# One core, layer norm, a scan and a gated feed-forward: up weights loaded row tile by row tile

## The chip, the cores and the metric

The kernel runs on one NeuronCore of a Trainium2 chip. The metric is the device time of one execution in microseconds (us): 178.7 us is the median of three runs of the kernel before, which lie between 178.48 and 179.15. Lower is better. The engines are TensorE (PE, with its weight loads PEld), VectorE (DVE), ScalarE (ACT), GpSimd (POOL) and SyncE (SP), whose queue issues nearly all DMAs here.

## What is computed

x is [2048, 512] in bfloat16. It is normalised over its 512 columns, then goes through two branches whose results are multiplied and added to x:

```python
xn = _layernorm(x, axis=-1)
s = _A_ref(xn, ...)          # h = Lam_bar*h + B_bar xn_t, y = 2 Re(C h) + xn*Dskip
g = _silu(_B_ref(xn, w_gate, w_up, w_down))
return x + s * g

def _B_ref(x, w_gate, w_up, w_down):
    return (_gelu(x @ w_gate) * (x @ w_up)) @ w_down
```

Branch A is a complex diagonal recurrence over the 2048 rows with 512 states, branch B a feed-forward of 1376 hidden columns.

## The kernel before, in words

The 2048 rows are cut into four slabs of 512 (NS = 4), each slab into four row tiles of 128 (M = 4). The 512 input columns are four row tiles of the weights (KT = 4, called k, rows 0 to 3 here), and the 1376 hidden columns are three chunks CH: 512, 512 and 352. W1 = 512 and W2 = 1024 are the ends of the first two.

For slab 0 the centred rows are transposed on TensorE (head_t, lines 378 to 402) into xcT, which lies in the tile W, and the up and gate products read it with the row scale put on at eviction. up_rows (lines 454 to 465) is one matmul, for row tile m, weight row k and chunk c; the four k of one (m, c) accumulate in one PSUM bank, and the last evicts it through out_up (L471, ScalarE). first_w (L499) does all four k of one (m, c) at a stretch, for the up chunks that up_rows leaves and for the gate weights wg (first_gates). In the kernel before up_rows takes the two wide chunks alone, and the 352-column chunk of all four row tiles goes through first_w.

For slabs 1 to 3 the normed rows are transposed by a DMA (dma_t4, L436) into xnT, and gate_tile (L536, evictions L539) computes up and gate products. Down products are L564 (down_pair; their SiLU is L567), with the gated rows transposed by a DMA (at_t, L551) into atT. half (L615, evictions L617) is the input product of the recurrence with BT; the rotations (L627, L635, L639) and the scans (L646) follow on VectorE. y_part (L579, L585, L586) is the output product with the C matrices, the two element-wise steps and the store (L589).

Loads: load_x (L296) brings one row tile of slab 0, load_w (L287) a part of wu or wg, load_slab (L291) a whole slab of x, L762 and L763 the down weights, L314, L436, L551 and L807 are DMA transposes. Before any of them TensorE runs seven dummy matmuls (L375).

The order of all work is written out by hand: every piece is registered with Plan.add in program order, and Plan.run emits the pieces in the order of the table ORDER, with buffers and PSUM banks given by SLOTS (six banks "ps", two "pp"). Each engine executes its own instructions strictly in that order. Numbers such as the end and landing times given to dma_sp, costs and ranks are arguments that Plan.add takes and does not use. The DMAs of SP and ACT share eight completion semaphores in turn, so a DMA waits on SP's queue until the eighth DMA before it has landed.

The order of SP's first loads before: x tiles 0, 1, 2; wu row 0 in two 512 chunks; the 352 chunk of all four rows in one load; wu row 1 first chunk; x tile 3; wu row 1 second chunk, row 2 first chunk, row 3 both wide chunks in one, row 2 second chunk; wg columns 512 to 1375, wg columns 0 to 511; slab 1; Drow; then the transposes.

Of the kernel before, what the change touches and what calls it, by code (L numbers as in the profile page):

```python
# [51 lines left out]
    ),  # L52
    "pp": (
        0, 1, 0, 1, 0, 1, 0, 1, 0, 0, 0, 1, 0, 1, 0, 1, 0, 1, 0, 1, 1, 0, 1, 0, 1, 1, 1, 0, 0, 0, 0, 1, 1, 0, 1, 0, 1, 0, 1,
    ),
    "U": (
        0, 1, 0, 2, 0, 1, 0, 2,
    ),
    "g2": (
        5, 0, 1, 4, 3, 0, 4, 2, 2, 0, 1, 5, 3, 1, 4, 5,  # L60
    ),
    "at": (
        2, 0, 1, 3, 2, 1, 0, 0, 0, 1, 2, 3, 2, 3, 0, 1,
    ),
    "gtA": (
        0, 0, 1, 1, 0, 1, 0, 1, 1, 0, 0, 0, 1, 1, 0, 0,
    ),
    "gtB": (
        1, 1, 0, 0, 0, 0, 1, 1, 1, 0, 0, 0, 0, 1, 0, 1,
    ),  # L70
    "ubA": (
        0, 1, 0, 0, 1, 1, 1, 0, 0, 0, 1, 1,
    ),
    "ubB": (
        0, 0, 1, 1, 1, 0, 0, 1, 0, 0, 1, 0,
    ),
    "yg": (
        0, 0, 1, 1, 0, 1, 0, 1, 0, 1, 1, 0, 0, 0, 1, 0, 1, 0,
    ),
    "ot": (  # L80
        1, 1, 1, 0, 1, 0, 0, 0, 0, 0, 0, 1, 1, 0, 1, 0, 1,
    ),
    "sk": (
        2, 3, 0, 1, 5, 7, 4, 6, 0, 1, 3, 2, 5, 4, 6, 7,
    ),
    "atT": (
        0, 1, 3, 0, 1, 1, 3, 2, 0, 3, 2, 1, 1, 2, 3, 0,
# [61 lines left out]
def kernel(  # L149
# [140 lines left out]
    def load_slab(s, **kw):  # L290
        dma(SP, 0.8, 4.0, lambda: nc.sync.dma_start(out=x_tok[:, s * M : (s + 1) * M, :], in_=x_r[:, s * M : (s + 1) * M, :]),  # L291
            writes=[("x", s, m) for m in range(M)], svc=SLAB, **kw)
# [8 lines left out]
    load_x(2, 2.06, 3.75)  # L301
    load_w("wu", 0, 1, 0, W1, 2.53, 4.4)
    load_w("wu", 0, 1, W1, W2, 3.0, 4.95)
    load_w("wu", 1, 2, 0, W1, 3.47, 5.5)
    load_w("wu", 1, 2, W1, W2, 3.94, 6.05)
    load_x(3, 4.41, 6.6)
    load_w("wu", 2, 3, 0, W1, 4.88, 7.15)
    load_w("wu", 2, 3, W1, W2, 5.35, 7.7)
    load_w("wu", 3, 4, 0, W2, 5.82, 8.8)
    load_w("wu", 0, KT, W2, F, 6.29, 10.0)  # L310
    load_w("wg", 0, KT, W1, F, 6.76, 12.4)
    load_w("wg", 0, KT, 0, W1, 7.23, 14.0)
# [141 lines left out]
    def up_rows(m, k, c):  # L454

        a, b = CH[c]
        if (m, c) not in opened:
            opened[m, c] = bank(m == 3)
        key, ps = opened[m, c]

        def f():
            T.matmul(ps[:], lhsT=xcT[:, k, m * P : (m + 1) * P], rhs=wu[:, k, a:b], start=(k == 0), stop=(k == KT - 1))  # L462
        pe(1, 512, f, [("xcT", m, k // 2), ("wu", k, c)], [key])
        if k == KT - 1:
            out_up(m, c, ps, key)
# [90 lines left out]
    def down_pair(s, h):  # L556
        for m in (2 * h, 2 * h + 1):
            key, ps = bank()
            gT, iT = atTs[s, m]

            def f(iT=iT, ps=ps):
                for k in range(NFT):
                    fs = min(P, F - k * P)
                    T.matmul(ps[:], lhsT=atT[:fs, k, iT * P : (iT + 1) * P], rhs=wd[:fs, k, :], start=(k == 0), stop=(k == NFT - 1))  # L564
            pe(NFT, 512, f, [("atT", gT), "wd0", "wd"], [key])
            g, i = g2s[s, m] = pl.group("g2")
            acts(512, lambda i=i, ps=ps: act(out=g2[i][:], in_=ps[:], func=AF.Silu), [key], [("g2", g)], table="silu", rank=3.0)  # L567
# [165 lines left out]
    up_rows(0, 0, 0)  # L733
    up_rows(0, 0, 1)
    head_t(2)
    for c in range(2):
        up_rows(1, 0, c)
    up_rows(0, 1, 0)
    up_rows(1, 1, 0)
    for c in range(2):  # L740
        up_rows(2, 0, c)
    for m in range(2):
        up_rows(m, 1, 1)
    for c in range(2):
        up_rows(2, 1, c)
    head_t(3)
    for c in range(2):
        for m in range(3):
            up_rows(m, 2, c)
    for k in range(3):  # L750
        for c in range(2):
            up_rows(3, k, c)
    for m in range(M):
        for c in range(2):
            up_rows(m, 3, c)
    for m in range(M):
        first_w("wu", m, 2)
# [4 lines left out]
    dma(SP, 0.6, 6.7, lambda: nc.sync.dma_start(out=wd[:, 0 : NFT - 1, :], in_=wd_r), writes=["wd0"], after=sp_last, svc=(2, 3.7, 1.0))  # L762
# [60 lines left out]
    def norm(s):  # L823
        if s > 1:
            load_slab(s, after=turned)
# [94 lines left out]
```

## Time and profile before

| | us |
|---|---|
| median of three runs (178.48 to 179.15) | 178.7 |
| span of the profiled execution | 176.9 |
| TensorE busy | 172.1 |
| VectorE busy | 154.6 |
| ScalarE busy | 132.6 |
| GpSimd busy | 10.9 |

The time of a run goes from the start of the program to its end on the device; the span goes from the first to the last instruction of the profiled execution, and 1.8 us of the median lie around it. Busy times are sums over the instructions of an engine; matmuls are pipelined and their shown length is latency, so the distance from one start to the next is the better measure. A row of the timeline gives start, length, engine, line, operation, what it writes and reads, and the count; a row of the chain of waits gives start, length and what the end of the kernel hung on at that time. The clock that TensorE was granted is 1.00 in every stretch.

### The profile page before, as it was taken

The numbers are of one execution on the slowest core, as the hardware profiler recorded it, in microseconds if no ns is written. First come the engines' busy times: TensorE is split into PE (matmuls) and PEld (weight loads), VectorE is DVE, ScalarE is ACT, GpSimd is POOL, SyncE is SP. The second block draws the span as 40 slices with busy tenths as digits, with TensorE's granted clock in tenths as the row PEclk, the third lists the DMA queues.
The fourth block names the chain that finished last, engine by engine and source line by source line (L and its number), as shares of the span: only waits on it lengthen the run. The fifth ranks groups of instructions, "written<-read, shape, count | busy, mean of one in ns | idle before, by whom it ended". The sixth has DMA issues, their size and how long they took to land.

```text
span 176.9 us, 2418 instructions
## 1 busy us (share of the span) xinstructions
PE 172.1 (97%) x834; PEld 82.3 (47%) x849; DVE 154.6 (87%) x253; ACT 132.6 (75%) x246; POOL 10.9 (6%) x25
## 2 busy tenths in 40 slices
PE   8999999999999999999999999999999999999992
PEld 2554544454454444444444444444444444444451
DVE  3743799999999988999999699999999999999343
ACT  6679999989999999956697665735898860793310
POOL 2640500000200000011000000000000000000000
PEclk9999999999999999999999999999999999999999
DMA  5999999997092730040057050063007300550531
GB/s 150 285 347 247 160 288 189 305 217 158 8 193 43 138 62 4 0 82 0 0 115 150 2 111 0 0 126 70 0 11 154 87 0 4 129 123 0 113 119 30
DMA packets 48467, 18.66 MB, mean 105 GB/s; under 512 B 40296, under 2 KB 48328, under 8 KB 48456
## 3 DMA queue, kind: packets, MB, share of 16 engines
q1 hardware_dynamic: 48432, 18.52, 46.7%
q8 instruction: 6, 0.10, 0.2%
q14 instruction: 5, 0.04, 0.1%
q10 hardware_dynamic: 24, 0.00, 0.0%
HBM read 6.46 MB, written 2.10 MB: 48 GB/s over the span
## 4 chain that ended last, share of the span: by engine, by line
PE 94%; DMA 2%; SPq 1%; issue 1%; DVE 0%
PE bank L536 31%; PE bank L564 21%; PE bank L615 16%; PE bank L579 16%; PE bank L499 7%; PE bank L462 3%; DMA wu<-in_B_w_up_dram 2%; SPq L296 1%; SPq L287 0%; DVE yg L585 0%; DVE ot L586 0%; PE bank L400 0%
## 5 line engine op out<-in xcount | busy, mean ns | idle before, releaser
L536 PEld LDWEIGHTS <-xnT 128*128 128x128 bf16 x288 | 28.1, 98 | 29.4
L564 PE MATMUL bank<-wd,atT 128*128 128x512 bf16 (+1 forms) x174 | 40.2, 379 | 0.1
L536 PE MATMUL bank<-wu,xnT 128*128 128x512 bf16 (+1 forms) x140 | 31.9, 356 | 0.1
L536 PE MATMUL bank<-wg,xnT 128*128 128x512 bf16 (+1 forms) x139 | 31.7, 356 | 0.3
L615 PE MATMUL bank<-xnT,BT 128*128 128x512 bf16 x128 | 30.9, 379 | 0.1
L646 DVE TENSOR_TENSOR_SCAN Fs<-rho,ini,W 128x512 bf16<-128x512 f32 x24 | 29.8, 1272 | 0.1
L579 PE MATMUL bank<-C,hst 128*128 128x512 bf16 (+1 forms) x134 | 29.7, 366 | 0.1
L564 PEld LDWEIGHTS <-atT 128*128 128x128 bf16 (+1 forms) x176 | 17.2, 98 | 20.3
L539 ACT ACTIVATE ubA<-bank 128x512 bf16<-128x512 f32 x24 | 14.6, 614 | 8.8 <-PE bank L536 8.3
L617 ACT ACTIVATE U<-bank 128x512 bf16<-128x512 f32 x32 | 19.1, 622 | 1.7 <-PE bank L615 1.7
L579 PEld LDWEIGHTS <-hst 128*128 128x128 bf16 x136 | 13.3, 98 | 14.0
L615 PEld LDWEIGHTS <-BT 128*128 128x128 bf16 x128 | 12.5, 98 | 14.3
L627 DVE TENSOR_TENSOR Q<-U,tab 128x4096 bf16<-128x4096 bf16 x8 | 18.3, 2287 | 0.7 <-ACT tab L715 0.6
L539 ACT ACTIVATE gtA<-bank 128x512 bf16<-128x512 f32 x24 | 14.8, 616 | 5.3 <-PE bank L536 4.6
L627 DVE TENSOR_TENSOR Q<-Fs,tab 128x4096 bf16<-128x4096 bf16 x8 | 18.3, 2285 | 0.1
L567 ACT ACTIVATE g<-bank 128x512 f32<-128x512 f32 x16 | 9.2, 594 | 12.1 <-PE bank L564 12.1
L585 DVE TENSOR_TENSOR yg<-bank,g 128x512 bf16<-128x512 f32 (+1 forms) x17 | 11.1, 655 | 5.0 <-PE bank L579 4.6
L539 ACT ACTIVATE ubB<-bank 128x352 bf16<-128x352 f32 x12 | 5.7, 475 | 6.6 <-PE bank L536 5.5
L838 ACT ACTIVATE junk<-x_tok 128x512 bf16<-128x512 bf16 x16 | 10.2, 649 | 0.0
L499 PE MATMUL bank<-wg,W 128*128 128x512 bf16 (+1 forms) x47 | 9.7, 356 | 0.1
L843 ACT ACTIVATE xna<-x_tok,nb,rs 128x512 bf16<-128x512 bf16 x12 | 9.6, 876 | 0.0
L575 ACT ACTIVATE bank<-sk 128x512 f32<-128x512 bf16 (+1 forms) x17 | 9.5, 577 | 0.1
(121 smaller groups left out, 190.0 us busy)
## 6 DMA issues: line engine op xcount, KB each, us to landing
out_dram<-ot SPq DMA_DIRECT2D x15, 128.0 KB, 1.8
x_tok<-in_A_x_dram SPq DMA_DIRECT2D x3, 512.0 KB, 5.6
wd<-in_B_w_down_dram SPq DMA_DIRECT2D x1, 1280.0 KB, 7.1
wg<-in_B_w_gate_dram SPq DMA_DIRECT2D x1, 864.0 KB
wu<-in_B_w_up_dram SPq DMA_DIRECT2D x6, 128.0 KB, 3.3
x_tok<-in_A_x_dram SPq DMA_DIRECT2D x4, 128.0 KB, 2.2
wg<-in_B_w_gate_dram SPq DMA_DIRECT2D x1, 512.0 KB, 7.8
wu<-in_B_w_up_dram SPq DMA_DIRECT2D x1, 352.0 KB, 3.9
```

Source lines behind the costliest of these rows:

```text
L499: T.matmul(ps[:, 0 : b - a], lhsT=xcT[:, k, m * P : (m + 1) * P], rhs=wt[:, k, a:b], start=(k == 0), stop=(k == KT - 1))
L536: T.matmul(ps[:, 0 : b - a], lhsT=xnT[:, s % 2, m, k, :], rhs=wt[:, k, a:b], start=(k == 0), stop=(k == KT - 1))
L539: acts(b - a, lambda: act(out=dst, in_=ps[:, 0 : b - a], func=AF.Copy if up else AF.Gelu_apprx_tanh), [key], [ok], table=None if up else " ...
L564: T.matmul(ps[:], lhsT=atT[:fs, k, iT * P : (iT + 1) * P], rhs=wd[:fs, k, :], start=(k == 0), stop=(k == NFT - 1))
L579: T.matmul(ps, lhsT=hst[s % 2][:, j // NPT, j % NPT, m * P : (m + 1) * P], rhs=C2[:, j // NPT, j % NPT, c0:c1], start=False, stop=(j == 2 ...
L585: dve(w, lambda: V.tensor_tensor(out=yg[iy][:, 0:w], in0=ps, in1=g2[ig][:, c0:c1], op=ALU.mult), [key, ("g2", gg)], [("yg", gy)])
L615: T.matmul(ps[:], lhsT=BT[:, ri, k, pt * P : (pt + 1) * P], rhs=xnT[:, s % 2, :, k, :], start=(k == 0), stop=(k == KT - 1))
L617: acts(512, lambda q=q, ri=ri, ps=ps: act(out=U[ui][:, ri, q, :], in_=ps[:], func=AF.Copy), [key], [("U", ug, q, ri)])
L627: dve(4096, lambda: V.tensor_tensor(out=Qf, in0=src.unsqueeze(1).to_broadcast(WQ), in1=table, op=ALU.mult), reads, ["Q"], rate=2.0)
L646: pl.add(DVE, 1.12 if s == 0 else 1.185, lambda ri=ri, q=q, pt=pt, first=first: V.tensor_tensor_scan(out=Fs[:, ri, q, :], data0=rho[:, pt ...
L838: acts(512, lambda i=i, fn=fn, sc=sc, m=m: act(out=junk()[:], in_=x_tok[:, s * M + m, :], func=fn, scale=sc, accum_out=sx[:, s, i, m : m + ...
L843: acts(512, lambda m=m: act(out=xn[m], in_=x_tok[:, s * M + m, :], func=AF.Identity, scale=rs[:, s, m : m + 1], bias=nb[:, s, m : m + 1]), ...
```

## The change

The up weights are loaded by row tile: row 0 in two parts (512 columns, then 864), rows 1 to 3 whole (1376 columns); x tiles 2 and 3 are loaded after row 0 and after row 2. up_rows takes the 352 chunk too, for row tiles 0 and 1, and the wide chunks of row tile 2; the 352 chunk of tile 2 and all of tile 3 go through first_w. Slabs 2 and 3 and the first ten row tiles of the down weights come in two loads each. The tables ORDER and SLOTS are new throughout, so the order of every engine's instructions is another; their numbers are left out here.

```diff
+    def load_slab(s, parts=1, **kw):
+        w = M // parts
+        for m0 in range(0, M, w):
+            a, b = s * M + m0, s * M + m0 + w
+            dma(SP, 0.8, 4.0, lambda a=a, b=b: nc.sync.dma_start(out=x_tok[:, a:b, :], in_=x_r[:, a:b, :]),
+                writes=[("x", s, m) for m in range(m0, m0 + w)], svc=SLAB, **kw)
...
     load_x(0, 1.12, 2.92)
     load_x(1, 1.59, 3.35)
-    load_x(2, 2.06, 3.75)
-    load_w("wu", 0, 1, 0, W1, 2.53, 4.4)
-    load_w("wu", 0, 1, W1, W2, 3.0, 4.95)
-    load_w("wu", 1, 2, 0, W1, 3.47, 5.5)
-    load_w("wu", 1, 2, W1, W2, 3.94, 6.05)
-    load_x(3, 4.41, 6.6)
-    load_w("wu", 2, 3, 0, W1, 4.88, 7.15)
-    load_w("wu", 2, 3, W1, W2, 5.35, 7.7)
-    load_w("wu", 3, 4, 0, W2, 5.82, 8.8)
-    load_w("wu", 0, KT, W2, F, 6.29, 10.0)
-    load_w("wg", 0, KT, W1, F, 6.76, 12.4)
-    load_w("wg", 0, KT, 0, W1, 7.23, 14.0)
+    load_w("wu", 0, 1, 0, W1, 2.06, 3.85)
+    load_w("wu", 0, 1, W1, F, 2.53, 4.75)
+    load_x(2, 3.0, 5.1)
+    load_w("wu", 1, 2, 0, F, 3.47, 6.1)
+    load_w("wu", 2, 3, 0, F, 3.94, 7.1)
+    load_x(3, 4.41, 7.5)
+    load_w("wu", 3, 4, 0, F, 4.9, 9.3)
+    load_w("wg", 0, KT, W1, F, 5.4, 12.9)
+    load_w("wg", 0, KT, 0, W1, 5.9, 14.3)
...
-            opened[m, c] = bank(m == 3)
+            opened[m, c] = bank(m == 2)
...
-            T.matmul(ps[:], lhsT=xcT[:, k, m * P : (m + 1) * P], rhs=wu[:, k, a:b], start=(k == 0), stop=(k == KT - 1))
-        pe(1, 512, f, [("xcT", m, k // 2), ("wu", k, c)], [key])
+            T.matmul(ps[:, 0 : b - a], lhsT=xcT[:, k, m * P : (m + 1) * P], rhs=wu[:, k, a:b], start=(k == 0), stop=(k == KT - 1))
+        pe(1, b - a, f, [("xcT", m, k // 2), ("wu", k, c)], [key])
...
     head_t(1)
+    for m in range(2):
+        for c in range(3):
+            up_rows(m, 0, c)
     head_t(2)
+    for k in range(1, KT):
+        for m in range(2):
+            for c in range(3):
+                up_rows(m, k, c)
+        if k == 1:
+            for c in range(2):
+                up_rows(2, 0, c)
+        for c in range(2):
+            up_rows(2, k, c)
     head_t(3)
+    first_w("wu", 2, 2)
+    for c in range(3):
+        first_w("wu", 3, c)
     for m in range(M):
         first_gates(m)
...
-    dma(SP, 0.6, 6.7, lambda: nc.sync.dma_start(out=wd[:, 0 : NFT - 1, :], in_=wd_r), writes=["wd0"], after=sp_last, svc=(2, 3.7, 1.0))
+    for i, (k0, k1) in enumerate(((0, NFT // 2), (NFT // 2, NFT - 1))):
+        dma(SP, 0.5, 4.0, lambda k0=k0, k1=k1: nc.sync.dma_start(out=wd[:, k0:k1, :], in_=wd_r[:, k0:k1, :]), writes=[f"wd{i}"],
+            after=sp_last, svc=(2, 1.85, 1.0))
...
-            load_slab(s, after=turned)
+            load_slab(s, parts=2, after=turned)
```

More of the change, by code (lines that the diff above doesn't have):

```diff
@@ L48 @@
     "ps": (
[3 rows of a table removed]
[3 rows of a table added]
     ),
     "pp": (
-        0, 1, 0, 1, 0, 1, 0, 1, 0, 0, 0, 1, 0, 1, 0, 1, 0, 1, 0, 1, 1, 0, 1, 0, 1, 1, 1, 0, 0, 0, 0, 1, 1, 0, 1, 0, 1, 0, 1,
+        0, 0, 1, 0, 1, 1, 0, 0, 0, 1, 1, 0, 0, 0, 1, 0, 1, 1, 0, 1, 0, 1, 1, 0, 0, 1, 1, 1, 0, 1, 1, 1, 1, 1, 0, 0, 0,
     ),
     "U": (
-        0, 1, 0, 2, 0, 1, 0, 2,
+        1, 0, 2, 1, 0, 2, 0, 1,
     ),
     "g2": (
-        5, 0, 1, 4, 3, 0, 4, 2, 2, 0, 1, 5, 3, 1, 4, 5,
+        2, 0, 1, 4, 2, 0, 5, 3, 2, 0, 1, 4, 5, 1, 3, 2,
     ),
     "at": (
-        2, 0, 1, 3, 2, 1, 0, 0, 0, 1, 2, 3, 2, 3, 0, 1,
+        0, 3, 1, 2, 1, 2, 0, 3, 3, 1, 0, 2, 0, 0, 1, 3,
     ),
     "gtA": (
-        0, 0, 1, 1, 0, 1, 0, 1, 1, 0, 0, 0, 1, 1, 0, 0,
+        0, 0, 1, 1, 1, 1, 0, 0, 1, 1, 0, 0, 1, 0, 1, 1,
     ),
     "gtB": (
-        1, 1, 0, 0, 0, 0, 1, 1, 1, 0, 0, 0, 0, 1, 0, 1,
+        1, 0, 1, 0, 0, 1, 0, 1, 0, 0, 1, 1, 1, 1, 0, 0,
     ),
     "ubA": (
-        0, 1, 0, 0, 1, 1, 1, 0, 0, 0, 1, 1,
+        1, 0, 1, 0, 1, 1, 0, 0, 1, 1, 0, 0,
     ),
     "ubB": (
-        0, 0, 1, 1, 1, 0, 0, 1, 0, 0, 1, 0,
+        0, 0, 1, 0, 1, 1, 1, 0, 1, 1, 0, 0,
     ),
     "yg": (
-        0, 0, 1, 1, 0, 1, 0, 1, 0, 1, 1, 0, 0, 0, 1, 0, 1, 0,
+        0, 1, 0, 1, 0, 0, 1, 0, 1, 1, 1, 0, 0, 0, 1, 0, 0, 1,
     ),
     "ot": (
-        1, 1, 1, 0, 1, 0, 0, 0, 0, 0, 0, 1, 1, 0, 1, 0, 1,
+        0, 1, 0, 1, 1, 1, 0, 0, 0, 1, 1, 1, 1, 1, 0, 1, 0,
     ),
     "sk": (
-        2, 3, 0, 1, 5, 7, 4, 6, 0, 1, 3, 2, 5, 4, 6, 7,
+        0, 1, 2, 3, 5, 6, 7, 4, 1, 7, 2, 0, 6, 3, 5, 4,
     ),
     "atT": (
-        0, 1, 3, 0, 1, 1, 3, 2, 0, 3, 2, 1, 1, 2, 3, 0,
+        2, 0, 1, 3, 3, 2, 0, 1, 3, 0, 1, 1, 2, 1, 2, 3,
     ),
@@ L288, in load_w @@
                [(nm, k, c) for k in range(k0, k1) for c in range(3) if c0 <= CH[c][0] < c1])
-    def load_slab(s, **kw):
-        dma(SP, 0.8, 4.0, lambda: nc.sync.dma_start(out=x_tok[:, s * M : (s + 1) * M, :], in_=x_r[:, s * M : (s + 1) * M, :]),
-            writes=[("x", s, m) for m in range(M)], svc=SLAB, **kw)
+    def load_slab(s, parts=1, **kw):
[4 more added lines that the diff above has]
+                writes=[("x", s, m) for m in range(m0, m0 + w)], svc=SLAB, **kw)
     def load_x(m, end, landed):
@@ L564, in f @@
                     T.matmul(ps[:], lhsT=atT[:fs, k, iT * P : (iT + 1) * P], rhs=wd[:fs, k, :], start=(k == 0), stop=(k == NFT - 1))
-            pe(NFT, 512, f, [("atT", gT), "wd0", "wd"], [key])
+            pe(NFT, 512, f, [("atT", gT), "wd0", "wd1", "wd"], [key])
             g, i = g2s[s, m] = pl.group("g2")
@@ L732 @@
     head_t(1)
-    up_rows(0, 0, 0)
-    up_rows(0, 0, 1)
+    for m in range(2):
+        for c in range(3):
+            up_rows(m, 0, c)
     head_t(2)
[L736 to L745, printed above, removed]
-    head_t(3)
[L747 to L757, printed above, removed]
+    for k in range(1, KT):
[7 more added lines that the diff above has]
+            up_rows(2, k, c)
+    head_t(3)
+    first_w("wu", 2, 2)
+    for c in range(3):
+        first_w("wu", 3, c)
     for m in range(M):
```

54 rows, old and new, of tables (ORDER, SLOTS) are left out of this document.

## The prediction, written before the changed kernel ran

> **What bounds the kernel now.** I read the head of the page first, then the chain of waits in order of time, then TensorE's timeline of the first 7 us. The page:
>
> ```profile
> span 176.9 us, 2418 instructions
> ...
> PE 172.1 (97%) x834; PEld 82.3 (47%) x849; DVE 154.6 (87%) x253; ACT 132.6 (75%) x246; POOL 10.9 (6%) x25
> ...
> PE 94%; DMA 2%; SPq 1%; issue 1%; DVE 0%
> ```
>
> TensorE is busy for 97% of the span and 94% of the chain that ends last is its matmuls. What is left in that chain is one DMA wait of 2%, and the chain in order of time (start, length, what) says where it lies:
>
> ```profile
> 3.06 3.89 DMA wu<-in_B_w_up_dram
> 6.95 0.04 issue
> 6.99 1.35 PE bank L499 x8
> ...
> 8.78 0.60 PE bank L499 x4
> 9.38 0.86 PE bank L462 x4
> 10.24 0.22 PE bank L400 x4
> ...
> 23.80 6.04 PE bank L615 x28
> ...
> 32.44 0.81 PE bank L536 x5
> ...
> 48.64 2.38 PE bank L564 x11
> ...
> 172.01 1.76 PE bank L579 x16
> 173.77 0.03 issue
> ```
>
> From 6.99 to 173.77 us nothing but TensorE stands in the chain, so a change that keeps TensorE's work can win only before 6.99, and loses wherever it makes a new gap. The same rows give the pace: a 512-column matmul 0.215 us (0.86 / 4), a 352-column one 0.15 (0.60 / 4), a transpose 0.055 (0.22 / 4). TensorE's timeline of the head (start, us, what):
>
> ```profile
> 3.90 0.66 PE L387 MATMUL bank<-ident,xna 128*128 128x128 bf16 x4
> 4.60 0.40 PE L400 MATMUL bank<-ident,xna 128*128 128x128 bf16 x4
> 4.84 0.38 PE L462 MATMUL bank<-wu,W 128*128 128x512 bf16 x1
> 5.21 0.40 PE L400 MATMUL bank<-ident,xna 128*128 128x128 bf16 x4
> 5.67 1.25 PE L462 MATMUL bank<-wu,W 128*128 128x512 bf16 x5
> ```
>
> Before 6.99 it issues 12 transposes and 6 matmuls of 512 columns, 12 x 0.055 + 6 x 0.215 = 1.95 us of work, and two tiny ones that both kernels have. From 3.90 to 6.99 are 3.09 us, so about 1.1 us is waiting: for the first two x tiles to be centred, which the change leaves alone, and from about 6.75 for the 352-column parts of all four up rows, one load issued at 3.06 that lands at 6.95.
>
> **The change, part by part.** The built program of the changed kernel holds the same 849 matmuls, so TensorE's work is equal and the sum is one of gaps.
>
> *Rows in place of columns.* TensorE's new order is: transposes of x tiles 0 and 1; row 0 for tile 0 (512, 352, 512 columns) and tile 1 (352, 512, 512); then a wait for row 1. Up to there nothing earlier moves: x0 and x1 are still the first two loads. VectorE's copy of tile 1 sets the rest of the start:
>
> ```profile
> 5.07 0.42 DVE L402 COPY W<-bank 128x512 bf16<-128x512 bf16 x1
> ```
>
> Tile 0 starts at 4.84 as now and takes 0.215 + 0.15 + 0.215 with some 0.09 of the tiny pair, to 5.51; tile 1's copy ends at 5.49 and its three parts (0.58) end at 6.09. That is when row 1 is wanted. Row 1 is loaded behind 128 KiB each of x0, x1, row 0's first part and x2, 216 KiB of row 0's rest, and is 344 KiB itself: 1072 KiB. What the loads do now:
>
> ```profile
> wu<-in_B_w_up_dram SPq DMA_DIRECT2D x1, 352.0 KB, 3.9
> wu<-in_B_w_up_dram SPq DMA_DIRECT2D x1, 128.0 KB, 3.8
> x_tok<-in_A_x_dram SPq DMA_DIRECT2D x1, 128.0 KB, 3.6
> ...
> 2.11 1.93 SPq L287 DMA_DIRECT2D wu<-in_B_w_up_dram  x4
> 4.08 0.43 SPq L296 DMA_DIRECT2D x_tok<-in_A_x_dram  x1
> ```
>
> (KB and us to landing of the third and fourth up load and of x3; then when the queue issues them.) The four up loads are issued 0.475 us apart, so the fourth, of 128 KB, goes out at 3.54 and lands at 7.34; the 352 KB one, with which 992 KiB are in, at 6.95. 1072 KiB lie between: 6.95 + 80/128 x 0.39 = 7.2. That is the late end for row 1. At the early end it is there when wanted, 6.09. Neither is excluded: the late end has the narrow 704-byte runs ahead of it, which the change takes away. I take the middle, 6.6. By then the new order has issued 8 transposes, four 512s and two 352s, 0.44 + 0.86 + 0.30 = 1.60 us, which is 0.35 less than the 1.95 that stand before 6.99 now. So the net of this step is 6.6 - 6.99 + 0.35 = 0.0 us, with the ends -0.55 and +0.55.
>
> [...]
>
> *x3 behind row 2.* The next waits come in the order row 2, x3's transposes, row 3. Between the row 1 wait and row 2 stand 4 transposes, four 512s and two 352s, 1.38 us (0.22 + 0.86 + 0.30), and row 2 is 352 KB (344 KiB) at the rates of the stretch:
>
> ```profile
> 0.00:4.00 4.00, 3.24 (x9) 1.00 (x9) 1.25 (x11) 2.51 (x6) 1.12 (x9) 1.00 0.52 141
> 4.00:5.00 1.00, 0.95 (x9) 0.45 (x8) 0.85 (x4) 1.00 (x5) 0.00 (x0) 1.00 0.78 194
> 5.00:6.00 1.00, 1.00 (x9) 0.54 (x9) 0.84 (x4) 1.00 (x4) 0.36 (x2) 1.00 1.02 323
> 6.00:7.00 1.00, 0.94 (x6) 0.30 (x5) 0.75 (x3) 0.45 (x2) 1.00 (x2) 1.00 1.05 357
> 7.00:8.00 1.00, 1.00 (x7) 0.67 (x7) 0.56 (x3) 0.16 (x1) 0.83 (x3) 1.00 1.01 262
> ```
>
> (The last figure is GB/s.) At 320 GB/s row 2 takes 1.1 us: hidden, and 0 to 0.1 late at the 262 of the last row. Then four 512s and two 352s, 1.16 us, so x3's transposes are wanted at 6.6 + 2.54 = 9.14. x3 now stands behind 1544 KiB (1.58 MB) instead of 1248 (1.28 MB). By the rows 1.08 MB have moved by 6.0, 1.28 MB by 6.55, and x3 landed at 4.08 + 3.6 = 7.7, 1.1 later; 1.58 MB have moved by 7.55, so x3 lands at 8.65 at the late end. After landing it needs its mean on ScalarE and its centring on VectorE:
>
> ```profile
> 8.29 0.62 ACT L423 ACTIVATE junk<-x_tok 128x512 bf16<-128x512 bf16 x1
> ...
> 9.14 0.35 DVE L424 TENSOR_SCALAR xna<-x_tok,ma 128x512 bf16<-128x512 bf16 x1
> ```
>
> 8.29 to 9.49 is 1.2 us, so its transposes can start at 9.85 and TensorE, which waits in order with rows 2, 3 and all gate work queued behind, loses 0.7; at the early end 0. I take 0.35. Row 3 is wanted 0.22 + 0.65 after those transposes and has by then had 3.5 us for 836 KB behind row 1, 2.6 us at 320 GB/s: hidden.
>
> *Slabs 2 and 3 and the down weights in two loads; the order of the rest.* Each half adds one issue of some 0.5 us on SP's queue, which waits for transposes anyway. Ahead of the transpose of slab 1's normed rows now stand slab 2 and half of slab 3, 256 KiB less than now; the down weights move behind the C matrices:
>
> ```profile
> 25.91 2.98 SPq L436 DMA_TRANSPOSE xnT<-xna  x1
> 28.94 0.59 SPq L762 DMA_DIRECT2D wd<-in_B_w_down_dram  x1
> ...
> xnT<-xna SPq DMA_TRANSPOSE x1, 4.9
> ...
> wd<-in_B_w_down_dram SPq DMA_DIRECT2D x1, 1280.0 KB, 7.1
> ```
>
> Slab 1's transpose lands at 30.8 and is first read at 32.44 (L536); the new order reads it 4 matmuls sooner, 0.86 us, which leaves 0.8 us of cover. The down weights land at 36.0 and are first read at 48.64 (L564), 12.6 us of cover. I take 0 for both; without cover the first costs its lateness one for one, since gate matmuls, ScalarE's evictions and the scans stand behind it.
>
> *The new order and ScalarE's tables.* The changed program loads ScalarE's tables 19 times instead of 15, and the first one of the down stage stands as ScalarE's 93rd instruction, not its 104th:
>
> ```profile
> L567 ACT ACT_TABLE_LOAD x7 | 9.0, 1283 | 0.1
> ...
> 28.00:60.00 32.00, 31.84 (x156) 15.28 (x158) 31.25 (x61) 31.09 (x67) 1.01 (x1) 1.00 0.73 154
> ...
> 100.00:160.00 60.00, 59.74 (x287) 28.37 (x291) 58.46 (x71) 40.52 (x66) 0.00 (x0) 1.00 0.28 60
> ```
>
> (Busy us of PE, PEld, DVE, ACT.) The four more, 4 x 1.28 = 5.1 us, stand late in the order, where ScalarE has 19.5 of 60 us free: 0. The early one falls towards the end of 28 to 60, where it has 0.9 of 32 free. The cost is 0 to 1.28; eight banks let ScalarE fall several groups of 0.86 us behind before TensorE waits, so I take 0.
>
> **The sum.** 0.0 + 0.35 + 0 + 0 = +0.35, taken as +0.3: span 176.9 + 0.3 = 177.2. The median of the runs shown, 178.7, lies 1.8 over the profiled span, so the forecast is 179.0 us, no difference that can be told: half a per cent, 0.9 us, is about what a measurement of this kernel can tell from no change.
>
> **The rivals.**
> 1. *The rows stream ahead of TensorE.* Row 1 is there at 6.09 and x3 in time: -0.55, 178.15. For it speaks the 194 GB/s between 4 and 5 us, a stretch in which small loads left the DMA engines idle; against it the 1.1 us by which landings trail the bytes moved. That is also the ceiling of any gain, 0.3%.
> 2. *The table load in the full stretch* (the other side). One more table load at the 93rd place pushes ScalarE's evictions back by 1.28 us while it has no idle time to recover; where it is over 0.4 us behind the banks' reserve, TensorE pays the rest, up to 0.3 + 1.28 = +1.6, 180.3. For it: ScalarE 31.09 of 32 us busy; against: the chain names no ScalarE wait now, and later it has room to catch up.
> 3. *Both late ends in the head*: +0.55 + 0.7 = +1.25, 179.95. For it: slow first landings as of the load at 3.06; against: that one had the narrow runs.
> 4. *Loads cost by the piece.* Each load pays its latency of some 2.2 us afresh, so whole rows land early, but the extra piece of slab 2 pushes slab 1's transpose 2.2 us back, 1.4 past its 0.8 of cover: -0.55 + 1.4 = +0.85, 179.55. The row for the latency is this one:
>
> ```profile
> x_tok<-in_A_x_dram SPq DMA_DIRECT2D x4, 128.0 KB, 2.2
> ```
>
> Against it: the loads at 3.54 and 4.08 land 0.34 us apart, not 2.2. [...]
>
> **How the numbers follow.** Forecast 0.56, rivals 0.12, 0.19, 0.08, 0.05. The forecast's own range is 178.4 to 179.7. The range of 8 in 10 takes in the ceiling of the gain and the table load: 178.1 to 180.5. Slower by over 0.5% (above 179.6): rivals 2 and 3, half of 4 and 0.04 of the forecast, 0.33. Faster by over 0.5% (below 177.8) lies past the ceiling, so only the scatter of the runs gives it: 0.05. Within: 0.62.
>
> **What would show it.** Right: in the chain the 3.89 us wait of up weights gives way to a wait for row 1 that ends between 6.1 and 7.2, a short gap before x3's transposes near 9.4, and unbroken TensorE from there to some 174.1. Rival 1 shows no DMA wait after 6.1; rival 2 ScalarE evictions in the chain between 45 and 65 us; rival 4 a gap before the first L536. The forecast falls if gaps elsewhere, which no row of the old order can show, add over 0.6 us: VectorE, busy 58.46 of 60 us, is where a new order could make one unseen.

## The result, and the profile after

The changed kernel takes 179.82 us (median of 5, 179.38 to 180.56) against 178.70 (178.47 to 179.15) for the kernel before on the same chip: a ratio of 1.0063, 95% interval 1.0035 to 1.0090. The prediction said 179.0 and no difference that can be told. The time lies in its range of 178.1 to 180.5, but above the forecast's own range, which ended at 179.7, and on the slower side: the interval leaves 1 out, so a loss of some 0.6% can be told.

The profiled execution has a span of 178.0 us, 1.1 longer than before. The page, with the shares of the chain that ended last in its last line:

```profile
span 178.0 us, 2418 instructions
...
PE 171.7 (96%) x833; PEld 82.3 (46%) x849; DVE 155.3 (87%) x253; ACT 138.0 (78%) x250; POOL 10.4 (6%) x25
...
PE 93%; DMA 3%; SPq 1%; issue 1%; DVE 0%
```

TensorE's busy time is the same within 0.4 us; its share of the chain fell by a per cent, and DMA's rose by one. The chain in order of time (start, length, what) has the place:

```profile
3.07 4.58 DMA wu<-in_B_w_up_dram
7.65 0.04 issue
7.70 0.53 PE bank L462 x2
8.22 0.22 PE bank L400 x4
8.44 1.96 PE bank L462 x10
10.40 0.22 PE bank L400 x4
10.62 1.29 PE bank L462 x6
...
32.04 0.60 PE bank L499 x4
32.63 0.22 PE bank L536
...
173.10 1.76 PE bank L579 x16
174.86 0.02 issue
```

The wait for the 352-column parts, which ended at 6.95, has become a wait for row 1, which ends at 7.65. From 7.70 to 174.86 there is TensorE and nothing else, as there was from 6.99 to 173.77. So the whole loss is made before x3's transposes (the four of line 400 at 10.40) and nothing behind them costs anything: from their end to TensorE's last matmul are 174.86 - 10.62 = 164.24 us, and before 173.77 - 10.46 = 163.31. The loss of 1.09 us is 0.16 by which these transposes end later, and 0.93 of matmuls that had been done ahead of them and now are not (twelve of 352 columns stood ahead of them before, six do now; six are 0.90 at the pace of 0.15). TensorE's timeline of the head (start, us, what, and in brackets the idle time ahead and what ended it):

```profile
5.39 0.97 PE L462 MATMUL bank<-wu,W 128*128 128x512 bf16 x4
7.70 0.53 PE L462 MATMUL bank<-wu,W 128*128 128x352 bf16 x2 [1.33 <-DMA wu<-in_B_w_up_dram]
8.06 0.39 PE L400 MATMUL bank<-ident,xna 128*128 128x128 bf16 x4
8.28 2.12 PE L462 MATMUL bank<-wu,W 128*128 128x352 bf16 x10
10.24 0.39 PE L400 MATMUL bank<-ident,xna 128*128 128x128 bf16 x4
```

The last matmul of row 0 for tiles 0 and 1 ends at 6.37 (7.70 - 1.33), and then TensorE stands until row 1 is whole. Row 1's load among the DMA issues (KB, us from issue to landing):

```profile
wu<-in_B_w_up_dram SPq DMA_DIRECT2D x1, 344.0 KB, 4.6
```

And what the DMA engines moved in these stretches (the last figure of a row, GB/s):

```profile
0.00:4.00 4.00, 3.24 (x9) 0.99 (x9) 1.09 (x5) 2.54 (x6) 1.15 (x9) 1.00 0.49 132
4.00:5.00 1.00, 0.80 (x9) 0.45 (x8) 0.57 (x3) 0.97 (x5) 0.00 (x0) 1.00 1.06 300
5.00:6.00 1.00, 1.00 (x8) 0.50 (x7) 0.60 (x3) 0.96 (x3) 0.24 (x1) 1.00 0.92 256
6.00:7.00 1.00, 0.37 (x2) 0.09 (x1) 0.96 (x3) 0.00 (x0) 0.79 (x1) 1.00 0.90 295
```

Up to 6.0 us 4 x 132 + 300 + 256 = 1084 KB had moved, and before the change 4 x 141 + 194 + 323 = 1081. As many bytes had moved; row 1's landing came later. If the loads moved strictly one after the other, row 1's last byte would be the 1098th KB (1072 KiB), moved by about 6.05 at this pace, and the load counts as landed at 7.65, 1.6 us behind. They don't: a load counts as landed with the last of sixteen updates of its semaphore, and in the trace the first update of row 2 comes at 6.74 and that of x3 at 7.07, ahead of row 1's last. Part of what had moved by 7.65 was theirs.

The second wait that was predicted, for x3, does not show. Its sums on ScalarE and its centring on VectorE:

```profile
9.06 0.63 ACT L423 ACTIVATE junk<-x_tok 128x512 bf16<-128x512 bf16 x1 [3.09 <-DMA x_tok<-in_A_x_dram]
...
9.82 0.35 DVE L424 TENSOR_SCALAR xna<-x_tok,ma 128x512 bf16<-128x512 bf16 x1 [0.91 <-ACT junk L423]
```

x3 landed at 8.97, and its centring ended at 10.17 (9.82 + 0.35). In the traces in which its transposes wait for it (e1, e2, e4, e8) they start 1.25 to 1.26 us after the landing; here that would be 10.23. By the timeline they start at 10.24, straight behind the matmul ahead of them. (The chain counts a piece from the end of the one before it, and matmuls overlap: hence its 10.40.) So in this trace the two paths that meet at x3's transposes arrive together, within a few hundredths: row 1's landing + 2.59 us, nearly all of it matmuls, and x3's landing + 1.26. The expectations below put the first at 2.74, which runs to the end of the matmul ahead and is 0.15 too long to be set beside 1.26. The experiments turn on these two paths.

### The profile page after: what moved, and what is told of

The parts are those of the page before. It is cut to its first block, busy times and chain, and to the rows that moved or that the text cites. A ratio compares the mean times of both kernels' runs of the same rounds, so it can differ in the third digit from the quotient of the medians.

```text
span 178.0 us, 2418 instructions
## 1 busy us (share of the span) xinstructions
PE 171.7 (96%) x833; PEld 82.3 (46%) x849; DVE 155.3 (87%) x253; ACT 138.0 (78%) x250; POOL 10.4 (6%) x25
## 4 chain that ended last, share of the span: by engine, by line
PE 93%; DMA 3%; SPq 1%; issue 1%; DVE 0%
PE bank L536 31%; PE bank L564 21%; PE bank L615 16%; PE bank L579 15%; PE bank L499 7%; PE bank L462 3%; DMA wu<-in_B_w_up_dram 3%; SPq L299 1%; SPq L287 0%; PE bank L400 0%; DVE yg L585 0%; DVE ot L586 0%
## 5 line engine op out<-in xcount | busy, mean ns | idle before, releaser
L832 ACT ACTIVATE junk<-x_tok 128x512 bf16<-128x512 bf16 x16 | 10.6, 687 | 0.0
```

Of the source, the lines that this page charges most:

```text
L832: acts(512, lambda i=i, fn=fn, sc=sc, m=m: act(out=junk()[:], in_=x_tok[:, s * M + m, :], func=fn, scale=sc, accum_out=sx[:, s, i, m : m + ...
```

## The experiments

Times are medians, ratios against the kernel before on the same chip, with 95% intervals in brackets. Numbers in the diffs of the order are steps: 4 and 7 load x2 and x3, 5, 6 and 8 the up rows 1, 2 and 3; 44 and 46 centre x2 and x3 on VectorE, 70 and 106 are their transposes, 71 is the copy of x2's, 79 and 81 x2's first matmuls, 77, 76, 74, 72, 75 and 73 row 1's, 84 to 87 row 2's. All traces in one table, in us: when the last byte of row 1, of row 2 and of x3 was counted as landed, when x3's transposes ended, and when TensorE's last matmul ended (a dash where the loads are cut otherwise or the trace has no landing).

```
                            row 1   row 2    x3    transposes   TensorE
                                                    of x3 end     end
before                        -       -     7.64      10.46     173.77
the change                  7.65    8.50    8.97      10.62     174.86
e1  the change again        7.92    9.57    9.90      11.55     175.79
e2  rows in two             7.70      -     8.93      10.58     174.82
e3  slabs, wd whole         7.48    8.36    8.74      10.45     174.68
e4  x2's work in the wait   7.05    8.87    9.27      10.92     175.16
e5  x3 ahead of row 2       7.54    8.76    7.86      10.51     174.78
e6  e5, x2's transposes     7.82    9.08    8.16      10.67     174.90
e7  e5, rows in two         6.94    9.00    7.93      10.44     175.82
e8  x3 behind row 3         7.66    9.14   10.32      11.97     176.21
e9  row 1 in three          6.85    9.84      -       11.87     177.30
e10 x2 behind row 1         7.03    8.20    8.60      12.30     176.53
e11 before, with halves       -       -     7.91      10.72     174.03
e12 e10 in a better order   6.15    8.29    8.63      10.62     175.15
```

**e1, the change unaltered, once more.**

> The changed kernel a second time. Theory A (one lost wait: TensorE's wait for row 1 of the up weights is the whole loss, 7.70 - 6.99 + 0.35 = 1.06 us) expects one DMA wait in the chain of waits, for row 1, ending between 7.2 and 8.2, no gap of TensorE behind it, and a time of 179.4 to 180.5, with end minus row-1 landing the same 167.2 us as in the first profile (174.86 - 7.66). Theory B (the loss is spread over the new order of the middle, and the head only happens to be of the same size) expects that difference to move by over 0.3 us.

180.15 us, ratio 1.0073 (1.0052 to 1.0094). The loss is confirmed. In this execution x3's path decides; its chain:

```profile
1.64 2.70 DMA wu<-in_B_w_up_dram
4.34 0.02 issue
4.36 5.55 DMA x_tok<-in_A_x_dram
...
9.99 0.73 ACT junk L423 x2
10.72 0.02 issue
10.74 0.36 DVE xna L424
11.11 0.05 issue
11.16 0.40 PE bank L400 x4
```

And TensorE's rows ahead of these transposes:

```profile
8.55 2.39 PE L462 MATMUL bank<-wu,W 128*128 128x352 bf16 x10
11.16 0.40 PE L400 MATMUL bank<-ident,xna 128*128 128x128 bf16 x4 [0.22 <-DVE xna L424]
```

Here x3's issue stood until row 0's first part had landed, at 4.34 (4.02 was its issue in the first trace). That is 0.34 of the 0.93 us by which x3 landed later, at 9.90; other loads were slower too: row 2, issued at 3.54 in both, landed 1.07 later. x3's transposes started 1.25 us after its landing, at 11.16, where row 1's path alone ends at 7.92 + 2.59 = 10.51. Of these 0.65 us some 0.27 is row 2 (the ten matmuls take 2.39 us instead of 2.12), the rest x3. The sign that was set for theory A therefore failed: from row 1's landing to TensorE's end are 167.87 us, not 167.2, a move of over 0.3 such as theory B had. But the middle of the kernel is not the cause, as theory B supposed: TensorE ends 164.24 us after the transposes, as in the first trace. So one kernel has two paths to x3's transposes, and which decides changes from execution to execution.

**e2, rows 1 to 3 in two loads each**, the columns from 512 on first.

```diff
-    load_w("wu", 1, 2, 0, F, 3.47, 6.1)
+    load_row(1, ((W1, F), (0, W1)), 3.47, 6.1)
...
+            for c0, c1 in cuts:
+                nc.sync.dma_start(out=wu[:, k : k + 1, c0:c1], in_=w_of["wu"][1][:, k : k + 1, c0:c1])
```

> Rows 1 to 3 each in two loads, columns 512 to 1375 first and then 0 to 511; the bytes and their order among the rows are the same. Theory A1 (row 1 is late by the bytes ahead of it) expects the 864 columns, which TensorE reads first, 128 KiB sooner than the whole row, some 0.4 us, so a row-1 wait that ends near 7.3 and a time of 179.4, with the whole row landing at 7.6 to 7.7 as now. Theory A2 (row 1 is late because loads of whole 2752-byte rows are slow to start, and the 16 DMA engines get apart: 1.85 us between the first and the last engine's completion) expects the second part too to land clearly sooner, 7.2 or before, first part 6.8, and a time of 178.9. Theory B expects 179.8.

180.13, ratio 1.0088 (1.0062 to 1.0114): no gain over the 180.15 of e1 on the same chip, so neither the 179.4 of theory A1 nor the 178.9 of A2. The whole row landed at 7.70, as A1 had it. The wait for row 1 shrank from 1.33 to 0.15 us and the time stayed. Its timeline says why:

```profile
7.74 2.13 PE L469 MATMUL bank<-wu,W 128*128 128x512 bf16 x9 [0.15 <-DMA wu<-in_B_w_up_dram]
10.19 0.40 PE L407 MATMUL bank<-ident,xna 128*128 128x128 bf16 x4 [0.32 <-DVE xna L431]
```

TensorE now waits for x3, which landed at 8.93: 8.93 + 1.26 = 10.19. One wait took the place of the other.

**e3, slabs 2 and 3 and the down weights whole again**, all else as in the change.

```diff
-  nc.sync.dma_start(out=x_tok[:, a:b, :], in_=x_r[:, a:b, :])
+  nc.sync.dma_start(out=x_tok[:, a:e, :], in_=x_r[:, a:e, :]) if m0 == 0 else None
-  nc.sync.dma_start(out=wd[:, k0:k1, :], in_=wd_r[:, k0:k1, :])
+  nc.sync.dma_start(out=wd[:, 0 : NFT - 1, :], in_=wd_r) if k0 == 0 else None
```

> Slabs 2 and 3 and the first ten row tiles of the down weights in one load each again, at the place of their first half; the head and the order of all engines stay as changed. Theory A expects no difference from the changed kernel: 179.5 to 180.2, chain unbroken after row 1. The theory that loads cost by the piece expects 0.3 us or more less than the changed kernel.

179.94, ratio 1.0065 (1.0044 to 1.0087), as the change itself. The halves carry none of the loss.

**e4, x2's transposes and one matmul of row 0 for tile 2 moved ahead of row 1's first matmul**, so that they fill the wait.

```diff
-  ..., 67, 68, 77, 76, 14, 44, 50, 51, 70, 20, 15, 71, ..., 85, 79, 86, ...
+  ..., 67, 68, 44, 70, 71, 79, 77, 76, 14, 50, 51, 20, 15, ..., 85, 86, ...
```

> The transposes of x tile 2 and one row-0 matmul of tile 2 are put ahead of the wait for row 1 (0.22 + 0.215 us of work that is ready by 7.1: tile 2 is centred at 6.35 in the profile of the changed kernel). Theory A expects exactly that much back: 179.82 - 0.44 = 179.4, with row 1 landing as before at 7.7. Theory B expects 179.8.

179.99, ratio 1.0066 (1.0048 to 1.0083), where 179.4 was expected: a miss. Row 1 landed at 7.05, earlier than in any other trace of this load order, and nothing waited for it:

```profile
7.38 2.64 PE L463 MATMUL bank<-wu,W 128*128 128x512 bf16 x12 [0.52 <-DVE W L403]
10.53 0.40 PE L401 MATMUL bank<-ident,xna 128*128 128x128 bf16 x4 [0.51 <-DVE xna L425]
```

TensorE stood 0.52 us for VectorE's copy of x2's transposes, which now had to be there first, and then 0.51 us for x3 (9.27 + 1.26 = 10.53). It was after these four that the theory of two paths was put down in numbers. Three theories went into the next runs: A, two paths of which the later decides; B, row 1 alone; C, the bytes of the head, so that whatever is brought forward makes something else late in its place.

**e5, x3's load ahead of row 2's, nothing else.**

```diff
-  ..., 4, 5, 6, 7, 8, 9, 10, 148, ...
+  ..., 4, 5, 7, 6, 8, 9, 10, 148, ...
```

> x tile 3 loaded ahead of up row tile 2, nothing else. Theory A (two paths end at x3's transposes, and what is after their end always takes TensorE 164.24 us: row 1's landing + 2.74 us of matmuls, and x3's landing + 1.26 us of sums and centring; the later one decides): x3 lands near 8.1 instead of 8.7 to 9.9, so its path is out of the way and row 1's path decides alone, x3's transposes start at 10.2 to 10.65; row 2 lands about where x3 did, 8.9 to 9.3, just ahead of its first use at row 1's landing + 1.64. TensorE ends at 174.7 to 175.1, median 179.7, a ratio of 1.005. Rival B (x3's path never mattered, the spread between executions is row 1's): no change, 179.95. Rival C (it is the bytes: whatever is put back ends late in x3's place): row 2's first matmul waits 0.3 to 0.6 us and the time stays at 179.95 to 180.2.

179.72, ratio 1.0049 (1.0032 to 1.0067), as A has it: x3 at 7.86, row 2 at 8.76, row 1's path alone (7.54 + 2.59 = 10.13; the transposes start at 10.12). It is the lowest median of the variants of the change, but its interval overlaps that of e1, and it is not shown to be better.

**e6, the same with x2's centring and transposes ahead of row 1's first matmul.**

```diff
-  ..., 68, 77, 76, 14, 44, 50, 51, 70, 20, 15, 71, 74, ...
+  ..., 68, 44, 70, 77, 76, 14, 50, 51, 20, 15, 71, 74, ...
```

> As e5, and x2's transposes put ahead of row 1's first matmul, so that they fill its wait. Theory A: row 1's path is shorter by the 0.22 us of four transposes, x3's is out of the way: x3's transposes start at 10.0 to 10.4, row 2 wanted at row 1's landing + 1.42; 0.2 under e5, 179.5, a ratio of 1.004. Rival B (row 1 alone, where filling its wait gave nothing in the run before): 179.9. Rival C: row 2 waits for what x3's transposes no longer wait for, 179.95.

179.97, ratio 1.0065 (1.0039 to 1.0092); A had 179.5. Row 1 landed at 7.82 in the trace, and from there to the start of x3's transposes were 2.46 us (10.28 - 7.82), only 0.12 less than in e5, because row 2, landed at 9.08, held TensorE for 0.10.

**e7, e5 with rows 1 to 3 in two loads.**

```diff
-    load_w("wu", 1, 2, 0, F, 3.47, 6.1)
+    load_row(1, ((W1, F), (0, W1)), 3.47, 6.1)
...
-  ..., 4, 5, 6, 7, 8, 9, 10, 148, ...
+  ..., 4, 5, 7, 6, 8, 9, 10, 148, ...
```

> Rows 1 to 3 in two loads each (columns 512 to 1376 ahead of 0 to 512), and x tile 3 ahead of row 2's loads. Theory A: row 1's first part lands at 6.65 and its second at 7.7 as in the run of rows in two, x3 at 8.1 instead of 8.93, so x3's path ends at 9.4 and row 1's at about 9.9; 0.3 us under the rows in two alone, 179.6, a ratio of 1.0045 or less. Rival B: 180.1 as the rows in two. Rival C: row 2's first part is late instead and the time stays, 180.0.

179.99, ratio 1.0070 (1.0045 to 1.0095); C's 180.0, not A's 179.6. Row 1 was whole at 6.94 and x3 there at 7.93, and row 2's first part, 8.70, became the wait:

```profile
8.74 1.48 PE L470 MATMUL bank<-wu,W 128*128 128x352 bf16 x6 [0.52 <-DMA wu<-in_B_w_up_dram]
```

The profiled execution is the longest of its six: it has a further wait of 1.0 us at 26 us, for a tile of ScalarE's, so TensorE ends 165.4 us after x3's transposes instead of 164.24. Whether more of its executions have it isn't known.

**e8, x3's load behind row 3's**, one place back.

```diff
-  ..., 4, 5, 6, 7, 8, 9, 10, 148, ...
+  ..., 4, 5, 6, 8, 7, 9, 10, 148, ...
```

> x tile 3 loaded behind up row tile 3, nothing else: 344 KB more ahead of it. Theory A and rival C: x3 lands at 9.8 to 10.9, its transposes start 1.26 us later, at 11.1 to 12.1, TensorE ends 0.7 to 1.0 us later than with the change, 180.7 to 181.0, a ratio of 1.011. Rival B (x3's path doesn't matter): 179.95.

180.95, ratio 1.0117 (1.0096 to 1.0137). A and C had 180.7 to 181.0, B 179.95; B is out. The chain has x3's path, with each step as long as in e1:

```profile
4.71 5.61 DMA x_tok<-in_A_x_dram
...
10.41 0.73 ACT junk L424 x2
...
11.17 0.36 DVE xna L425
...
11.58 0.40 PE bank L401 x4
11.97 1.29 PE bank L463 x6
```

**e9, row 1 alone in three loads** (runs of 1024, 704 and 1024 bytes in place of 2752), x3 ahead of row 2.

```diff
-    load_w("wu", 1, 2, 0, F, 3.47, 6.1)
+    load_row(1, ((W2, F), (W1, W2), (0, W1)), 3.47, 6.1)
...
-  ..., 4, 5, 6, 7, 8, 9, 10, 148, ...
+  ..., 4, 5, 7, 6, 8, 9, 10, 148, ...
```

> Row 1 alone in three loads in the order of use (columns 864 to 1376, 512 to 864, 0 to 512: runs of 1024, 704 and 1024 bytes per partition, as the kernel before has them) in place of runs of 2752 bytes, and x tile 3 ahead of row 2; the same bytes in the same order otherwise. Theory P (the long runs make row 1 late): its last part lands at 6.9 to 7.2, x3's transposes start at 9.7 to 9.95, 0.4 us under x tile 3 ahead alone, 179.3. Theory R (the bytes ahead of it at the rate of this stretch make it late): the last part lands at 7.4 to 7.8 as the whole row does (7.05 to 7.92 in eight traces); the first parts are used a little sooner, 179.5 to 179.7.

180.88, ratio 1.0131 (1.0090 to 1.0173). Row 1 was whole at 6.85, sooner than in any of the seven traces in which it is one load behind x2 (7.05 to 7.92, mean 7.59); so far as one trace goes, theory P. But the two more issues put row 2's at 5.08, it landed at 9.84, and TensorE stood for it:

```profile
9.88 1.57 PE L470 MATMUL bank<-wu,W 128*128 128x352 bf16 x6 [2.00 <-DMA wu<-in_B_w_up_dram]
```

That made a loss where both theories had a gain. What followed this long wait besides is told at the end.

**e10, x2's load behind row 1's**, with x2's transposes behind row 1's matmuls and row 2's first two.

```diff
-  ..., 41, 4, 5, 6, ..., 14, 44, 50, 51, 70, 20, 15, 71, 74, ..., 84, 85, 79, 86, ...
+  ..., 41, 5, 4, 6, ..., 14, 50, 51, 20, 15, 74, ..., 84, 85, 44, 70, 71, 79, 86, ...
```

> x tile 2 loaded behind up row 1 and its transposes put behind row 1's six matmuls and row 2's first two; so 128 KB less ahead of row 1. Theory R: row 1 lands 0.3 to 0.4 us sooner than the 7.6 it has on the mean, at 7.2 (6.7 to 7.55 with the spread between executions), x2 at about 7.65, in time for transposes at 8.9; then x3 (8.7 to 9.9 so far, + 1.26) decides, x3's transposes start near 10.2, and the time is 179.75, 0.2 or less under the change: the bytes of x3's path are the same. Theory P, or row 1's own load deciding its landing: row 1 at 7.5 or later, 179.95.

181.97, ratio 1.0171 (1.0135 to 1.0208). Row 1 landed at 7.03, in the span that R gave it. The time answers nothing on R, because the order was badly chosen: x2's centring came to stand behind x3's on VectorE, so x2, landed at 7.34, was transposed at 10.19.

**e11, the kernel before with halves alone**: slabs 2 and 3 and the down weights in two loads, up rows and order as before.

```diff
-  nc.sync.dma_start(out=x_tok[:, s * M : (s + 1) * M, :], in_=x_r[:, s * M : (s + 1) * M, :])
+  parts(x_tok, x_r, s * M, s * M + M, s * M + (M // 2 if s > 1 else M))
-  nc.sync.dma_start(out=wd[:, 0 : NFT - 1, :], in_=wd_r)
+  parts(wd, wd_r, 0, NFT - 1, (NFT - 1) // 2)
...
+        for i, j in ((a, cut), (cut, b)):
+            if i < j:
+                nc.sync.dma_start(out=dst[:, i:j, :], in_=src[:, i:j, :])
```

> The kernel before with the other part of the change alone: slabs 2 and 3 and the down weights in two loads each, the halves issued one behind the other; up rows, order and buffers as before. If the head carries the whole loss: 178.8 to 179.0 (0 to 0.1 us from before), TensorE unbroken from 7.0 us on. If the halves cost by the piece (rival 4 of the prediction): 1.4 us or more, 180.2.

179.26 against 178.85, ratio 1.0017 (1.0003 to 1.0030): within half a per cent, though 0.4 us, more than the 0.1 expected. In the trace the 352 KB load lands at 7.21 instead of 6.95, and behind x3's transposes TensorE takes 174.03 - 10.72 = 163.31 us, to the hundredth what it took before. So what there is lies in the head, where the two kernels do the same; why it should be later in the median stays open.

**e12, e10 in an order that can use it**: VectorE centres x2 ahead of x3, and x2's matmuls stand between row 2's and x3's transposes.

```diff
-  ..., 14, 50, 51, 20, 15, 74, ..., 73, 45, 46, 38, 48, 49, 84, 85, 44, 70, 71, 79, 86, 81, 87, 106, ...
+  ..., 14, 44, 50, 51, 20, 15, 74, ..., 73, 45, 48, 49, 84, 85, 70, 71, 46, 38, 86, 87, 79, 81, 106, ...
```

> x tile 2 loaded behind up row 1 as in the run before, with its steps now in an order that can use it: VectorE centres x2 ahead of x3 (the run before had x2's centring queued behind x3's), TensorE does row 1's six matmuls, row 2's first two, x2's transposes, row 2's other two for tile 1, x2's first two matmuls, then x3's transposes. Theory A (TensorE's end = end of x3's transposes + 164.24 us, and these start at the later of row 1's landing + 2.74 us and x3's landing + 1.26 us): with 128 KB less ahead, row 1 lands near 7.05 and x3 near 8.6 to 8.9, as in the run before, so x3's transposes start at 9.8 to 10.2, TensorE ends at 174.25 to 174.6, and the time is 179.45, a ratio of 1.0035; row 2's landing (8.2 to 8.5, wanted at row 1's + 1.3) may cost 0.1 of it. If the bytes of the head make the loss whatever their order (theory C): 179.9.

179.86, ratio 1.0051 (1.0035 to 1.0067): C's 179.9, not A's 179.45. With 128 KB less ahead of it row 1 landed at 6.15, in time, and TensorE ran through its six matmuls without a stop. Then:

```profile
5.40 2.13 PE L463 MATMUL bank<-wu,W 128*128 128x512 bf16 x10
8.34 0.53 PE L463 MATMUL bank<-wu,W 128*128 128x352 bf16 x2 [0.80 <-DMA wu<-in_B_w_up_dram]
...
9.79 0.61 PE L463 MATMUL bank<-wu,W 128*128 128x512 bf16 x2 [0.34 <-DVE W L403]
10.23 0.39 PE L401 MATMUL bank<-ident,xna 128*128 128x128 bf16 x4
```

It stood 0.80 us for row 2 and 0.34 for the copy of x2's transposes, which on VectorE had come behind 0.61 us of statistics, and x3's transposes end at 10.62, as in the change.

Together: in nine traces (the change, e1 to e6, e8 and e10) TensorE's end is the end of x3's transposes + 164.23 to 164.27 us, wherever these transposes lie. The three others add a cost of their own behind them: e7's wait, 0.3 us in e12, and 1.2 us in e9. Of the eight kernels made to bring row 1 or x3 forward or to fill the wait (e2, e4 to e7, e9, e10, e12) not one ends these transposes before 10.44 us, and e3, which left the head as it was, has 10.45: row 1, row 2 and x3 are all needed by then, and in these traces but e9's the last of them comes at 8.6 to 9.3. None beats the kernel before.

## Why the prediction was right, and where it was wrong

**What bounds it.** Right: the middle of the kernel is bound by TensorE, and all that happened lies ahead of 10.6 us. That a change could win only before 6.99 was not put to the test, since none of the kernels won; that it loses by the new gaps it makes held for every variant of the change.

**Rows in place of columns.** The formula was right and its input wrong. "Row 1's landing - 6.99 + 0.35" gives, with the 7.70 us at which TensorE went on, 1.06; the loss measured is 1.09, and the 2.54 us of matmuls from there to x3's transposes came out to the hundredth (7.70 to 10.24). The failed step is "I take the middle, 6.6", between row 1 there when wanted at 6.09 and a late end of 7.2. It was there at 7.65, and 7.48 to 7.92 in five more traces; only e4's 7.05 lies inside the bounds. When it is wanted was nearly right: the last four matmuls of row 0 start at 5.39 and take 0.80 at the pace, to 6.19 instead of 6.09.

The late end was itself too early. It came from bytes at the pace of the 352 KB load, which landed 1.1 us behind its bytes counted in the order of issue. By the same count row 1's landing trailed by 1.6. In the trace the sixteen updates of the load's semaphore come from 5.80 to 7.65, over 1.85 us, where those of the 352 KB load of before come from 5.82 to 6.95. Shown is that the landing depends on more than the bytes ahead; e9 (three shorter runs: 6.85) speaks for the length of the runs, e2 (two: 7.70) against it, e10 and e12 (128 KB less ahead: 7.03 and 6.15) for what is queued in front. How much each has is not settled, with single traces that differ by up to 0.9 us for the same load in the same place.

**x3 behind row 2.** Taken as 0.35, it cost nothing in the profile of the change, where it came just in time, and some 0.4 in that of e1. It landed at 8.97, or 9.90, where the late end was 8.65; the 1.2 us from landing to transposes were 1.26. Its price was not added to row 1's but lay under it. The sum added two waits that are ends of parallel paths, and what counts is the later of them; e2, e4 and e8 show this path deciding.

**Slabs, down weights and the order.** Zero was right: e3 takes the halves out and changes nothing (a ratio of 1.0065, the change 1.0063; the 0.4 us of e11 stay open). Slab 1's turned rows landed at 32.0 (issued at 27.25, 4.8 us) and were first read at 32.63, a cover of 0.6 where 0.8 was worked out. **ScalarE's tables.** Zero was right: the four more loads show as 138.0 us busy instead of 132.6, and the chain names no ScalarE.

**The rivals.** The outcome is nearest to rival 3, both late ends in the head, 179.95, to which 0.08 was given. Its ground for being unlikely was that the slow landing of the load at 3.06 came from its narrow runs; the load issued at that time now, 80 KiB further back and with runs some four times as long, landed 0.7 us later. That rival 3's number fits is luck. By the prediction's own steps its two late ends do not add: with row 1 at 7.2 x3's transposes are wanted at 7.2 + 2.54 = 9.74, so x3, ready at 9.85, costs 0.1 more and not 0.7, and the rival comes to 179.4. Row 1 then came 0.45 us behind its late end, where some 0.6 had been counted twice. Rival 1 (rows early), rival 2 (tables) and rival 4 (price by the piece) did not happen.

**The signs and the range.** Of the three signs of being right the last came: TensorE is unbroken behind x3's transposes, to 174.86 instead of 174.1. The wait for row 1 ended at 7.65, outside the 6.1 to 7.2, and there was no gap ahead of x3's transposes. The range held the result, but it reached to 180.5 for the table load, which cost nothing; the head alone, by its own bounds, ended at 179.95. "No difference that can be told" was too strong: the loss is small but clear of the scatter, and "slower by over 0.5%" had been given 0.33.

## What to carry to other kernels

A chain that is one engine from some point on splits the work: everything behind that point can be checked with one subtraction (here 164.23 to 164.27 us in nine traces), and the study can keep to what lies ahead. Where loads feed the start of a kernel, reckon a load as usable only when its last update comes, leave room beyond the bytes (here landings came 1.1 and 1.6 us behind them, and that of one load moved by up to 0.9 between executions), and write down for each wait the next one behind it: removing row 1's wait brought up x3's (0.32 us in e2), and bringing x3 forward brought up row 2's (0.52 in e7). Waits on paths that meet are compared, not added.

## What the runs showed of the hardware that was not expected

In the profiled execution of e9 the 2.00 us in which TensorE stood were followed by a loss of their own. In the windows of that trace (TensorE's busy time follows the length; the figure ahead of the last two is the granted clock):

```profile
8.00:9.00 1.00, 0.00 (x0) 0.00 (x0) 0.12 (x1) 0.87 (x3) 0.80 (x3) 1.00 0.83 304
9.00:10.00 1.00, 0.12 (x1) 0.10 (x1) 0.67 (x3) 1.00 (x3) 0.27 (x2) 1.00 1.00 340
10.00:11.00 1.00, 1.00 (x6) 0.44 (x5) 0.00 (x0) 0.26 (x2) 0.47 (x1) 0.91 0.97 360
11.00:12.00 1.00, 1.00 (x7) 0.68 (x6) 0.09 (x1) 0.00 (x0) 0.00 (x0) 0.50 1.05 374
...
13.00:14.00 1.00, 1.00 (x4) 0.40 (x3) 0.87 (x4) 0.32 (x1) 0.02 (x1) 0.50 1.06 365
14.00:15.00 1.00, 1.00 (x7) 0.50 (x5) 0.00 (x0) 1.00 (x3) 0.99 (x1) 0.88 1.09 361
```

The clock fell to 0.50 a microsecond after the wait had ended, and stayed there for some 3.4 us: 0.91 and 0.88 are the means of the two windows in which it changed, and worked out from them the half clock runs from about 10.82 to 14.24. TensorE's end shows the price behind x3's transposes: 177.30 - 11.87 = 165.43, 1.2 us more than the 164.24 of the others; the first six matmuls behind them take 2.53 us (11.87 to 14.40) where the same six take 1.29 in the change. In the profiled execution of e10 a wait of 1.42 us, and in the change one of 1.33, left the clock at 1.00.

Not every execution of e9 shows it. Two of its six, the profiled one among them, have a mean clock of 0.991 and take 182.5 and 182.9 us; the four others, at 0.998 to 1.000, take 180.6 to 181.0, so e9's median is nearly free of this cost. Of e10's six executions three, at 0.990 or 0.991, take 182.5 to 183.1 us and three, at 1.000, 181.0 to 181.5: its profiled execution is one that kept its clock, and its median of 181.97 lies between the two groups. What decides in which executions the clock falls is not shown.

The same load, issued at the same 3.07 us behind the same loads, landed anywhere from 7.05 to 7.92 us in seven traces. That is 0.87 us, not much less than the whole effect of the change.
